# Attention and gated convolution on one core: five of seven slots of P through the DMA transpose, v scaled in its cast, row sums inverted before their transpose

## The chip, the core and the metric

The kernel runs on one core of a Trainium2 chip. The core has a matrix engine (TensorE, PE in the profile; its weight loads are PEld), a vector engine (VectorE, DVE), a scalar engine (ScalarE, ACT), a general one (GpSimd, POOL) and SyncE (SP), which here only issues DMAs. They work side by side and wait for one another by semaphores. Operands lie in SBUF; TensorE writes to PSUM, which has eight banks. The metric is the device time of one launch in microseconds.

## What is computed

For 8 batches and 12 heads of 448 tokens with 64 dimensions, q and k are normalised by their root mean square and multiplied by a gain; softmax attention gives x; x (448 x 768 a batch) goes through a matrix of 768 x 1024, a relu, a convolution of three taps along the tokens, a sigmoid gate, and a matrix of 1024 x 768.

```python
q_n, k_n = (rmsnorm(q, g_q), rmsnorm(k, g_k))
scores = scale * np.matmul(q_n, k_n.transpose(0, 1, 3, 2))
scores = scores - np.max(scores, axis=-1, keepdims=True)
attn = np.exp(scores)
attn = attn / (np.sum(attn, axis=-1, keepdims=True) + 1e-09)
out = np.matmul(attn, v)
...
h = np.maximum(x @ w_in, 0.0)
conv_out[t] = conv_w[0] * h[t - 1] + conv_w[1] * h[t] + conv_w[2] * h[t + 1]
gate = 1.0 / (1.0 + np.exp(-conv_out))
return h * gate @ w_out
```

## The kernel before

**Precision.** Most products run in fp16 with operands split in a cast and a remainder (names ending in `_hi` and `_lo`), three matmuls for one: high by high and the two mixed ones. An operand is scaled by a power of two first, so that the cast is safe. What stays in f32 is multiplied in f32 directly.

**Pairs, slots, groups.** The 96 heads go in 48 pairs n, six a batch. The 896 query rows of a pair are seven slots of 128. `SLOTS` (567) gives the order in which the slots are worked (index j) and `GROUPS` (568) which of them share a group of score matmuls. The first three groups hold two slots each, one from each head, and use the two halves of 64 rows of TensorE at once; the last holds slot 3 alone, which has rows of both heads, and uses all 128 rows with the operand `qz`, which `q_middle` (484) copies together on POOL or DVE. For each slot `soft_max` (602) takes the row maximum on DVE and `soft_exp` (608) the exponential on ACT, which also sums the row into a column of `rsum`. The exponentials go to a ring `e` of three buffers.

**P, turned in two ways.** The product with v needs P transposed. In the pairs before `n1` = 8 all seven slots are transposed on TensorE in f32 (`p_transpose`, 648, line 651 in the profile) and copied from PSUM to `PT` by ACT or DVE (`p_evac`, 655). From pair 8 on, the first nd = 4 slots take another way: `p_hi` (626) casts P to fp16, `p_lo` (634) makes the remainder, both in one of three buffers `ph`, and `p_turn` (641) has SP issue a DMA transpose of both into the other part of `PT`. `pv` (715) multiplies: eight f32 products (line 723) over the columns of the slots that TensorE turned, 192 of each head's 448 columns from pair 8 on, and 24 fp16 matmuls (line 732) over the other 256. The fp16 part needs v split as well: `v_scaled` (694) multiplies v by its power of two in place, on POOL or DVE, `v_hi` (700) casts it, `v_lo` (703) subtracts. The scale comes from the largest absolute value of v in the batch (`v_scale`, 547), and is taken out again behind the convolution and at the output.

**The sums.** When all seven slots are summed, `rsum` (128 x 7) is transposed on TensorE to 7 x 128 (666), `sum_evac` copies it out of PSUM and adds 1e-9 (671), `sum_inverse` takes the reciprocal on DVE (663), and SP writes it to DRAM and reads it back twice, spread over 64 partitions each (`rB`, 676 and 682). `x_scale` (740) multiplies the product by it; `x_hi` and `x_lo` split x.

**The rest.** q and k are loaded, squared, summed and scaled (`square`, `square_sum`, `rsqrt`, `apply_rms`), then transposed on TensorE (458) or, for q from pair 8 on, by DMA (`x_turn`, 451). When a batch's six pairs are done, `in_part` (800, line 806) and `out_part` (869, line 883) multiply by the two weight matrices, with the relu, the convolution, the gate and a split between. The weights come as 64-bit floats, which DVE unpacks with integer operations (`to_f32`, 205); they are then scaled and split (`split` on ACT, `rest` on DVE or POOL).

**The order of the work.** A planner in the kernel gives each step a due time (`at`, 141): pair n begins at `base(n)` (68), which is `T0` for each of the first `N0` pairs and `T` after that; other steps are due at fixed distances from it, and the weights between `wi0` and `wi1`, `wo0` and `wo1` (the constants of line 20). `needs` (989) says what a step waits for and `options` (1253) which engines can do it and at what cost, `PATIENCE` (1331) what a second choice is charged. A loop simulates the engines, picks at each moment the most urgent step that can start, and so writes the fixed order of each engine's instructions. DVE operations named in `SHARED` (1432) are planned so as not to overlap POOL's. SP's queue is in order too: a transfer that waits holds those behind it.

## Time and profile before

| | us |
|---|---|
| median of 3 runs | 926.09 |
| lowest, highest | 924.29, 948.67 |
| the profiled execution | 925.0 |
| its span, from first to last instruction | 923.2 |
| TensorE busy in the span | 849.0 |
| DVE, ACT, POOL busy | 730.2, 667.4, 627.3 |

The mean clock granted to TensorE was 0.972 of full speed. In a row of the groups stand the source line, the engine, the operation, the tiles that it writes and reads with their shapes, the number of instructions, then the busy time, the mean of one in ns, and the idle time of the engine before them with what ended it. A row in order of time begins with its start and its length. A row of waits names who waited for whom, then the sum, the count and the longest. A line can be that of a helper: 78 is every plain copy and cast, 90 every two-operand operation, so there the tiles tell which step it is.

### The profile page before, as it was taken

The numbers are of one execution on the slowest core, as the hardware profiler recorded it, in microseconds if no ns is written. First come the engines' busy times: TensorE is split into PE (matmuls) and PEld (weight loads), VectorE is DVE, ScalarE is ACT, GpSimd is POOL, SyncE is SP. The second block draws the span as 40 slices with busy tenths as digits, with TensorE's granted clock in tenths as the row PEclk, the third lists the DMA queues.
The fourth block names the chain that finished last, engine by engine and source line by source line (L and its number), as shares of the span: only waits on it lengthen the run. The fifth ranks groups of instructions, "written<-read, shape, count | busy, mean of one in ns | idle before, by whom it ended". The sixth has DMA issues, their size and how long they took to land.

```text
span 923.2 us, 18519 instructions
## 1 busy us (share of the span) xinstructions
PE 849.0 (92%) x6430; PEld 508.7 (55%) x6430; DVE 730.2 (79%) x1336; ACT 667.4 (72%) x1525; POOL 627.3 (68%) x705
## 2 busy tenths in 40 slices
PE   1686687998999999999999999999999999999998
PEld 0343344555656566556665566566655666566554
DVE  6998987999788887798798976898789876893330
ACT  3677776887688776788688877787788867885441
POOL 2396887787699768668688857777778755872120
PEclk9897787999999999999999999999999999999999
DMA  8934432376885878556976588568696695455001
GB/s 212 259 96 126 122 113 63 89 135 117 185 147 130 156 152 170 123 117 124 187 148 139 115 182 168 95 135 164 150 170 126 119 175 120 84 94 112 18 18 52
DMA packets 296878, 120.18 MB, mean 130 GB/s; under 512 B 258048, under 2 KB 293200, under 8 KB 296784
## 3 DMA queue, kind: packets, MB, share of 16 engines
q1 hardware_dynamic: 296784, 119.00, 62.1%
q8 instruction: 50, 0.82, 0.4%
q14 instruction: 44, 0.36, 0.1%
HBM read 56.65 MB, written 11.18 MB: 73 GB/s over the span
## 4 chain that ended last, share of the span: by engine, by line
PE 67%; DVE 18%; DMA 5%; ACT 4%; issue 2%; SPq 2%; POOL 2%; DVEq 0%; ACTq 0%; POOLq 0%
PE bank L883 19%; PE bank L806 19%; PE bank L600 9%; PE bank L723 7%; PE bank L651 6%; PE bank L732 4%; DMA rB<-rd 3%; PE bank L462 2%; DVE rT L663 1%; DMA v<-in_v_dram 1%; DVE st L365 1%; DVE wo L214 1%; POOL sq L90 1%; DVE vacc L528 1%; SPq L643 1%
## 5 line engine op out<-in xcount | busy, mean ns | idle before, releaser
L806 PE MATMUL bank<-x,wi 128*128 128x448 f16 x1152 | 241.9, 354 | 0.3 <-ACT e_(8_0_1731 L614 0.3
L883 PE MATMUL bank<-wo,gring 128*128 128x384 f16 (+1 forms) x1056 | 205.4, 327 | 0.7 <-DVE c_(4_7_8185 L839 0.3
L806 PEld LDWEIGHTS <-wi 128*128 128x128 f16 x1152 | 110.2, 98 | 99.8 <-issue 14.7
L883 PEld LDWEIGHTS <-gring 128*128 128x128 f16 (+1 forms) x1056 | 101.8, 99 | 62.7 <-issue 11.0
L78 ACT COPY PT<-bank 112x512 f32<-112x512 f32 x166 | 96.6, 586 | 42.9 <-PE bank L651 41.9
L600 PE MATMUL bank<-kT,qT 64*128 64x448 f16 x864 | 107.1, 370 | 1.2 <-ACT qT L78 0.6
L90 POOL TENSOR_TENSOR sq<-qkf,st 112x512 f32<-112x512 f32 x79 | 87.5, 1125 | 17.6 <-DVE st L387 15.6
L723 PE MATMUL bank<-PT,v 112*64 112x192 f32 (+1 forms) x768 | 88.8, 374 | 1.7 <-ACT PT L78 1.3
L90 POOL TENSOR_TENSOR x<-rB,x 128x448 f16<-128x448 f32 x48 | 51.5, 1073 | 47.5 <-ACT x L78 36.4
L723 PEld LDWEIGHTS bank<-PT,v 112*64 112x64 f32 x768 | 51.5, 138 | 34.5 <-issue 18.1
L600 PEld LDWEIGHTS <-qT 64*128 64x128 f16 x864 | 34.8, 97 | 49.4 <-issue 28.2
L365 DVE TENSOR_REDUCE st<-sq 112x16 f32<-112x1024 f32 x48 | 57.9, 1207 | 3.7 <-ACT sq L357 3.6
L732 PE MATMUL bank<-PT,vp 112*64 112x256 f16 x960 | 59.2, 273 | 0.0
L696 POOL TENSOR_SCALAR v<-v,vsc 112x512 f32<-112x512 f32 x35 | 57.6, 1649 | 1.9 <-DVE vsc L200 0.9
L732 PEld LDWEIGHTS <-vp 112*64 112x64 f16 x960 | 53.0, 110 | 2.6
L741 DVE TENSOR_TENSOR rB<-bank,rB 128x448 f32<-128x448 f32 x48 | 29.7, 619 | 29.4 <-DMA rB<-rd 20.7
L491 POOL COPY qz<-qT 64x128 f16<-64x128 f16 x88 | 33.2, 378 | 28.3 <-DMA qT<-qkf 17.2
L462 PE MATMUL bank<-ident,sq 112*128 112x112 f32 x224 | 33.6, 276 | 18.8 <-POOL sq L90 18.7
L90 POOL TENSOR_TENSOR vp<-v,vp 112x512 f16<-112x512 f32 x39 | 46.6, 1195 | 2.8 <-ACT vp L78 1.6
L883 PE MATMUL bank<-wo,wi 128*128 128x384 f16 (+1 forms) x192 | 46.9, 326 | 0.0
L663 DVE RECIPROCAL rT<-rT 7x128 f32<-7x128 f32 x48 | 44.9, 935 | 0.7
L90 POOL TENSOR_TENSOR qkf<-sq,qkf 112x512 f16<-112x512 f32 x29 | 35.0, 1208 | 13.8 <-ACT qkf L78 7.2
(2235 smaller groups left out, 2101.6 us busy)
## 6 DMA issues: line engine op xcount, KB each, us to landing
qkf<-in_k_dram SPq DMA_DIRECT2D x48, 224.0 KB
qkf<-in_q_dram SPq DMA_DIRECT2D x48, 224.0 KB
v<-in_v_dram SPq DMA_DIRECT2D x48, 224.0 KB
rB<-rd SPq DMA_DIRECT2D x96, 112.0 KB
wo<-in_moe_w_in_dram SPq DMA_DIRECT2D x12, 512.0 KB
gring<-in_moe_w_out_dram SPq DMA_DIRECT2D x16, 384.0 KB
PT<-ph SPq DMA_TRANSPOSE x160
rd<-rT SPq DMA_DIRECT2D x48, 3.5 KB
```

The lines of the kernel that those rows point to most:

```text
L78: (nc.scalar.copy if e == "ACT" else elementwise(e).tensor_copy)(dst, src)
L90: elementwise(e).tensor_tensor(dst, a, b, op=op)
L365: nc.vector.tensor_reduce(old("st", m)[:, 0, n - m].rearrange("p i s -> p (i s)"), old("sq", n).rearrange("p i h t d -> p (i h t) d"), axi ...
L462: nc.tensor.transpose(ps[:, t * PB : (t + 1) * PB], x[:, t], ident[:PB, :PB])
L600: nc.tensor.matmul(ps[u][:, :S], lhs, kt[r, w], start=(i == 0), stop=(i == 2))
L651: nc.tensor.transpose(ps[:PB, kt * P : (kt + 1) * P], e[:, kt * PB : (kt + 1) * PB], ident)
L663: nc.vector.reciprocal(old("rT", n), old("rT", n))
L696: elementwise(on["v_scaled", n]).tensor_scalar(v, v, old("vsc", n // NP)[:PB, 1:2], None, op0=ALU.mult)
L723: nc.tensor.matmul(ps[HALF[h], out[h]], v[:, h, k], pt[:, k, col[h]], start=(k == 0), stop=(k == NB - 1),)
L732: nc.tensor.matmul(ps[HALF[h], out[h]], v[:, w, h, k], pt[:PB, a, k, col[h]], start=(i == 0 and k == 0), stop=(i == 2 and k == NB - 1),)
L806: nc.tensor.matmul(ps[:, :S], wi[:, wl, c, fc * P : (fc + 1) * P], old("x", b * NP + c)[:, xl], start=(i == 0), stop=(i == 3 * NP - 1),)
L883: nc.tensor.matmul(ps[p0 : p0 + m, :NO2], g, wo[:, wl, fc, half * NO2 : (half + 1) * NO2], start=(i == 0), stop=(i == 3 * NFC - 1),)
```

## The change

From pair 10 on instead of pair 8, five slots in place of four go through the DMA transpose (`dg` is now that number); the slots are worked in the order 2, 4, 1, 5, 3, 0, 6, so that 0 and 6, the first rows of one head and the last of the other, stay on TensorE. Slot 3 is now the fifth in the order, and its group the third of four. The f32 product covers 128 columns a head from pair 10 on, the fp16 one 320.

`v_scaled` is gone. The scale of v is applied in the cast (`v_hi`) and in the remainder, which is now always on DVE as (v x scale) - cast. The f32 product takes v as loaded, so its slots lack the scale: `sum_evac` multiplies the inverted sums by the scale for these slots and by one for the others, from a column of `vsc` that `v_scale` fills with one more small operation, from two masks made once in `prepare`.

The sums are completed (`sum_add`, on ACT, DVE or POOL) and inverted as 128 x 7, then transposed and evacuated.

The constants of the planner are changed with it (`T0` and `N0`, `T`, the weights' times, the charges of second choices), `x_cast`, `x_hi`, `in_hi` and `p_hi` may go to POOL too, `scores` waits for `q_middle` only in the group of slot 3, and options that were switched off (`xin`, `gin`, `ein`) are taken out.

```diff
-    T0=18.19, N0=5, T=16.2, ti=26.722, si=4.889, so=6.734, hop=0.568, beta=0.028, wi0=-41.512,
-    wi1=117.871, wo0=38.32, wo1=134.629, cw=-29.146, p_evac=1.201, p_hi=2.093, p_lo=5.553,
...
-    sp=0.107, nbulk=5, p_rs=0.005, p_sq=0.945, p_w=0.508, v0=-5.896, dg=2, n1=8, sw=0, pvs=4,
+    T0=16.073, N0=6, T=15.869, ti=26.722, si=4.889, so=6.219, hop=0.568, beta=0.028, wi0=-40.836,
+    wi1=117.871, wo0=31.379, wo1=166.21, cw=-27.026, p_evac=1.19, p_hi=1.894, p_lo=5.553,
...
+    p_ev=8.767, sp=0.066, nbulk=4, p_rs=0.005, p_sq=0.939, p_w=0.414, v0=-5.839, dg=5, n1=10,
+    sw=0, pvs=2, pk=0.1, p_sa=0.167, p_ph=0.399, p_pl=0.756, nq=8, nk=99, p_qh=0.524, p_ql=0.275,
...
     def v_scale(b):
...
         pow2_scale(sc[:, 0:1], sc[:, 1:2])
+        nc.vector.scalar_tensor_tensor(
+            sc[:NS, 6:7], raw_slot[:NS], sc[:NS, 1:2], cast_slot[:NS], op0=ALU.mult, op1=ALU.add
+        )
...
-    SLOTS = (0, 6, 1, 5, 2, 4, 3)
-    GROUPS = ((0, 1), (2, 3), (4, 5), (6,))
+    SLOTS = (2, 4, 1, 5, 3, 0, 6)
+    GROUPS = ((0, 1), (2, 3), (4,), (5, 6))
...
-        return 0 if n < PH["n1"] else 2 * PH["dg"]
+        return 0 if n < PH["n1"] else PH["dg"]
...
+    def sum_add(n):
+        r = old("rsum", n)
+        if on["sum_add", n] == "ACT":
+            nc.scalar.activation(r, r, AF.Identity, bias=tiny)
+        else:
+            elementwise(on["sum_add", n]).tensor_scalar(r, r, 1e-9, None, op0=ALU.add)
+
     def sum_inverse(n):
-        nc.vector.reciprocal(old("rT", n), old("rT", n))
+        nc.vector.reciprocal(old("rsum", n), old("rsum", n))
...
     def sum_evac(n):
-        nc.vector.tensor_scalar(
-            new("rT", n, [NS, P], F32), bank("t", ("r", n))[:NS, :P], 1e-9, None, op0=ALU.add
+
+        w = 6 if nd(n) else 1
+        copy_scaled(
+            on["sum_evac", n], new("rT", n, [NS, P], F32), bank("t", ("r", n))[:NS, :P],
+            old("vsc", n // NP)[:NS, w : w + 1],
         )
...
-    def v_scaled(n):
-        v = old("v", n).rearrange("p h t d -> p (h t d)")
-        elementwise(on["v_scaled", n]).tensor_scalar(
-            v, v, old("vsc", n // NP)[:PB, 1:2], None, op0=ALU.mult
         )
 
     def v_hi(n):
-        copy(on["v_hi", n], new("vp", n, [PB, 2, 2, NB, D], F16)[:, 0], old("v", n))
+        copy_scaled(
+            on["v_hi", n], new("vp", n, [PB, 2, 2, NB, D], F16)[:, 0], old("v", n),
+            old("vsc", n // NP)[:PB, 1:2],
+        )
 
     def v_lo(n):
         vp = old("vp", n)
-        binary(on["v_lo", n], vp[:, 1], old("v", n), vp[:, 0], ALU.subtract)
+        nc.vector.scalar_tensor_tensor(
+            vp[:, 1], old("v", n), old("vsc", n // NP)[:PB, 1:2], vp[:, 0], op0=ALU.mult,
+            op1=ALU.subtract,
+        )
...
         elif name == "scores":
             for h in range(2):
                 yield ("x_turn" if turned(n, h) else "qk_lo"), n, h
-                yield "q_middle", n, h
+                if a[1] == 2:
+                    yield "q_middle", n, h
```

More of the change, by code (lines that the diff above doesn't have):

```diff
@@ L611, in soft_exp @@
         c = SLOTS[j]
-        if not inside(n, j):
-            new("e", (n, j), [P, S], F32)
         nc.scalar.activation(
-            powers(n, j), bank("s", (n, j))[:, :S], AF.Exp, bias=old("sst", (n, j)),
+            new("e", (n, j), [P, S], F32), bank("s", (n, j))[:, :S], AF.Exp, bias=old("sst", (n, j)),
             accum_out=old("rsum", n)[:, c : c + 1],
         )
-    def inside(n, j):
-        return PH["ein"] and j < nd(n)
-    def powers(n, j):
-        return bank("s", (n, j))[:, :S] if inside(n, j) else old("e", (n, j))
     def p_hi(n, j):
@@ L735, in pv @@
                 )
-    def x_place(n):
-        return bank("m", ("v", n))[:, :S] if PH["xin"] else old("rB", n)
     def x_scale(n):
-        nc.vector.tensor_tensor(x_place(n), bank("m", ("v", n))[:, :S], old("rB", n), op=ALU.mult)
+        t = old("rB", n)
+        nc.vector.tensor_tensor(t, bank("m", ("v", n))[:, :S], t, op=ALU.mult)
     def x_hi(n):
-        copy(on["x_hi", n], new("x", n, [P, 2, S], F16)[:, 0], x_place(n))
+        copy(on["x_hi", n], new("x", n, [P, 2, S], F16)[:, 0], old("rB", n))
     def x_lo(n):
         xt = old("x", n)
-        binary(on["x_lo", n], xt[:, 1], x_place(n), xt[:, 0], ALU.subtract)
+        binary(on["x_lo", n], xt[:, 1], old("rB", n), xt[:, 0], ALU.subtract)
     def plan_attention(n):
@@ L1169, in needs @@
             yield "sum_store", n
[L1170 removed]
+            yield "x_lo", n - BUFS["rB"]
             if a[1]:
@@ L1339, in takes @@
         if name == "scores":
-            return "s", [((a[0], j), ("p_lo" if inside(a[0], j) else "soft_exp", a[0], j)) for j in GROUPS[a[1]]]
+            return "s", [((a[0], j), ("soft_exp", a[0], j)) for j in GROUPS[a[1]]]
         if name == "qk_transpose":
@@ L1350, in takes @@
             return "t", [(("x", a[0]), ("v_scale", *a))]
-        if name == "pv" and not a[1]:
-            return "m", [(("v", a[0]), ("x_lo" if PH["xin"] else "x_scale", a[0]))]
+        if name == "pv" and a[1] == pvs(a[0])[0]:
+            return "m", [(("v", a[0]), ("x_scale", a[0]))]
         if name == "in_part" and not a[-2]:
-            return "m", [(("i", *a[:2]), ("in_lo" if PH["gin"] else "in_gate", *a[:2]))]
+            return "m", [(("i", *a[:2]), ("in_gate", *a[:2]))]
         if name == "out_part" and not a[-2]:
@@ L1357, in takes @@
         if name == "in_conv" and not a[-1]:
-            return "c", [(None, ("in_gate" if PH["gin"] else "in_lo", *a[:2]))]
+            return "c", [(None, ("in_lo", *a[:2]))]
         if name == "out_evac":
@@ L1402, in mode @@
     def mode(name, *a):
-        return name if name == "pv" or name == "scores" and a[1] < NG - 1 else ""
+        return name if name == "pv" or name == "scores" and a[1] != 2 else ""
     taken = {step: takes(*step) for step in steps}
@@ L1432, in tile_attention_moe @@
     SHARED = (
-        "apply_rms", "apply_gain", "x_cast", "x_rest", "p_lo", "p_hi", "v_lo", "v_hi", "v_scaled",
+        "apply_rms", "apply_gain", "x_cast", "x_rest", "p_lo", "p_hi", "v_lo", "v_hi", "sum_add",
         "x_hi", "x_lo", "in_hi", "in_lo", "in_carry", "q_middle", "convert", "rest", "moe_scales", "rsqrt",
     )
-    shared = set(SHARED)
-    for key, names in dict(xin=("x_hi", "x_lo"), gin=("in_hi", "in_lo"), ein=("p_hi", "p_lo")).items():
-        if PH[key]:
-            shared -= set(names)
     port = dict(DVE=0.0, POOL=0.0)
     def locks(e, name):
-        return e == "POOL" or e == "DVE" and name in shared
+        return e == "POOL" or e == "DVE" and name in SHARED
     BULK = ("load", "load_k", "load_q", "v_load")
```

129 lines of the change are left out of this document (66 added, 63 removed).

## The prediction

> **What bounds the kernel now.** I read the first two parts of the page, then the busy times by stretch, then TensorE's rows in order of time, then the groups by line and the waits.
>
> ```profile
> span 923.2 us, 18519 instructions
> PE 849.0 (92%) x6430; PEld 508.7 (55%) x6430; DVE 730.2 (79%) x1336; ACT 667.4 (72%) x1525; POOL 627.3 (68%) x705
> q1 hardware_dynamic: 296784, 119.00, 62.1%
> ...
> 25.00:175.00 150.00, 114.80 (x643) 61.74 (x644) 134.99 (x250) 108.98 (x255) 111.85 (x118) 0.83 0.47 121
> 175.00:200.00 25.00, 25.00 (x174) 13.14 (x172) 24.63 (x42) 22.32 (x53) 23.26 (x31) 1.00 0.65 119
> 200.00:250.00 50.00, 45.15 (x363) 28.41 (x363) 43.66 (x86) 37.52 (x88) 36.30 (x37) 1.00 0.75 151
> 250.00:850.00 600.00, 590.84 (x4777) 364.21 (x4773) 493.66 (x901) 466.37 (x1071) 440.22 (x497) 1.00 0.71 139
> 850.00:923.00 73.00, 68.54 (x464) 39.23 (x462) 16.52 (x25) 24.00 (x43) 9.32 (x9) 1.00 0.09 34
> ```
>
> The columns of a stretch are its length, then the busy time of PE, PEld, DVE, ACT and POOL, the granted clock, the DMA share and GB/s. There are two regimes. From 250 to 850 us PE works 590.84 of 600 us at clock 1.00, while DVE has 18% left, ACT 22%, POOL 27%: there the span is PE's work. From 25 to 175 us PE stands idle for 150 - 114.80 = 35.2 us, its clock is 0.83, and DVE is busy for 134.99 of 150, the fullest of all: there DVE sets the pace, for it also unpacks and splits the weights. The profiled execution took 925.0 us, 1.8 more than its span and 1.1 less than the median of 926.09; the sum below is made against 925.0.
>
> **TensorE's terms.** Ends of matmuls are modelled and overlap, so I take distances between starts.
>
> ```profile
> 401.94 1.52 PE L723 MATMUL bank<-PT,v 112*64 112x192 f32 x16
> 403.29 1.48 PE L732 MATMUL bank<-PT,vp 112*64 112x256 f16 x24
> 404.71 0.74 PE L600 MATMUL bank<-kT,qT 64*128 64x448 f16 x6
> 405.38 1.88 PE L806 MATMUL bank<-x,wi 128*128 128x448 f16 x9
> ...
> 411.08 0.60 PE L651 MATMUL bank<-ident,e_(21_5_5148 128*112 128x128 f32 x4
> 411.52 1.30 PE L806 MATMUL bank<-x,wi 128*128 128x448 f16 x6
> ...
> 413.29 1.31 PE L600 MATMUL bank<-kT,qT 64*128 64x448 f16 x12
> 414.53 0.60 PE L462 MATMUL bank<-ident,sq 112*128 112x112 f32 x4
> ...
> 60.64 3.23 PE L723 MATMUL bank<-PT,v 112*64 112x448 f32 x16 [1.31 <-ACT PT L78]
> ```
>
> - A slot of P moved from PE to the DMA saves four transposes, 411.52 - 411.08 = 0.44 us. 38 pairs (10 to 47) send one more: -16.7. Pairs 8 and 9 send none instead of four: 8 x 0.44 = +3.5.
> - The f32 product of P and v falls from 192 to 128 columns a head. From 448 to 192 columns it fell by 3.23 - 1.52 = 1.71, 6.7 ns a column, so 64 fewer save 0.43: x38 = -16.2. Pairs 8 and 9 return to 448: 2 x 1.71 = +3.4. Should weight loads, which don't shrink, set part of the pace, the saving is less; its ends are 0 and 16.2.
> - The f16 product grows from 256 to 320 columns. It takes 404.71 - 403.29 = 1.42 now; in proportion +0.36, x38 = +13.5, and pairs 8 and 9 drop it: -2.8. Its ends are 0 (if weight loads set its pace) and 13.5; I take the upper, since 24 matmuls in halves of 256 columns have little else to wait for.
> - The full-height group of scores (the single slot) moves from last to third, so the half-height groups are split once more a pair. Twelve half-height matmuls in a row take 414.53 - 413.29 = 1.24, six take 405.38 - 404.71 = 0.67: a split costs 0.10, or 0 where other work already stood between. I take half: 48 x 0.05 = +2.4, ends 0 and 4.8. The f32 product is now issued in two steps (pvs 2); both are ready at once, so I expect them back to back, 0, with the same upper end of 4.8.
>
> [...]
>
> PE's sum is -16.7 + 3.5 - 16.2 + 3.4 + 13.5 - 2.8 + 2.4 = -12.9 us. The bounds above give -26.4 - 2.4 at the one end (f16 product free, no splits) and +5.7 at the other (f32 product saving nothing, every group split), neither likely, since weight loads that set the pace would hit both products, -12.9 + 16.2 - 13.5 = -10.2.
>
> **VectorE, GpSimd, ScalarE.**
>
> ```profile
> L663 DVE RECIPROCAL rT<-rT 7x128 f32<-7x128 f32 x48 | 44.9, 935 | 0.7
> L536 DVE TENSOR_SCALAR vsc<-vsc 128x1 f32<-128x1 f32 x8 | 1.2, 154 | 0.3
> L696 POOL TENSOR_SCALAR v<-v,vsc 112x512 f32<-112x512 f32 x35 | 57.6, 1649 | 1.9 <-DVE vsc L200 0.9
> L696 DVE TENSOR_SCALAR v<-v,vsc 112x512 f32<-112x512 f32 x13 | 7.2, 550 | 0.0
> L90 POOL TENSOR_TENSOR vp<-v,vp 112x512 f16<-112x512 f32 x39 | 46.6, 1195 | 2.8 <-ACT vp L78 1.6
> L90 DVE TENSOR_TENSOR vp<-v,vp 112x512 f16<-112x512 f32 x1 | 1.5, 1531 | 0.0
> L301 DVE SCALAR_TENSOR_TENSOR wo<-wo,wsc 128x768 f16<-128x768 f32 x8 | 9.6, 1203 | 1.7 <-ACT wo L293 1.6
> L214 DVE SCALAR_TENSOR_TENSOR wo<-gring,wo 128x384 int32<-128x384 int32 x16 | 12.7, 795 | 0.3
> ...
> L671 DVE TENSOR_SCALAR rT<-bank 7x128 f32<-7x128 f32 x48 | 13.2, 274 | 16.0 <-PE bank L666 15.9
> L78 ACT COPY PT<-bank 112x512 f32<-112x512 f32 x166 | 96.6, 586 | 42.9 <-PE bank L651 41.9
> ...
> 25.00:175.00 150.00, 6.89 (x8) 0.83 0.47 121
> ...
> 25.00:175.00 150.00, 17.91 (x10) 0.83 0.47 121
> ```
>
> The last two rows are the reciprocals on DVE and the scaling of v on POOL between 25 and 175 us.
>
> - Reciprocal: 935 ns for 128 elements a partition. With 7 a partition it lies between the 154 ns of the one-element row and 274, the next row of this chain; I take 0.2. Saving 48 x 0.735 = 35.3. The new addition of 1e-9 costs 0.15 (by the 154 ns) wherever it is put; the evacuation after the transpose replaces the one before it, 0.27 for 0.27.
> - Scaling of v: 57.6 on POOL and 7.2 on DVE go. The scale comes into the cast of v (a scaled copy instead of a copy, no change of length taken; ends 0 and +0.1 a pair) and into the evacuation of the sums.
> - Remainder of v: 46.6 leaves POOL; 38 come to DVE as an operation of two SBUF inputs and a scale. Nearest rows: 795 ns at 384 and 1203 at 768 columns, so 0.93 at 512; the single remainder already on DVE took 1.53. 38 x 0.93 = 35, ends 27 and 58.
> - Remainders of P: 30 more (190 for 160) at about 1.05, +31 on POOL; 30 more casts on ACT (0.56, in the next fence) replace 30 evacuations (0.59).
>
> After 175 us DVE thus changes by about -30 - 7 - 2 + 35 + 6 = +2 us, at the worst end +25, against 106 us free; POOL by -40 - 47 + 31 = -56, so it can take the casts that the planner may now send it. Nothing here becomes the bound, and I cost all of it at nothing: PE's matmuls cover it. So too the first two groups of scores, which need not wait for the middle copies any more (no row of PE's waits names these), and five small operations in the preparation, 0.15 us each, before PE's first work.
>
> **The start.** Eight reciprocals lie in 25 to 175 us: -5.9 on DVE, +1.2 for the additions, -4.7 in all. The due times spread the second weight matrix over 134.8 us instead of 96.3, from 31.4 in place of 38.3, in 26 steps; the remainders start 16.5 steps and 6 us in, now at 105, the last before pair 8's 139.6, and then at 123, against pair 8's 128.2, so that 7 of the 8 (1203 ns each) come due at pair 8 or after: 8.4 us moved to where DVE has room. POOL loses 17.9 there, which only makes it a freer helper. DVE's relief is 13.1 of 134.99 us. The products of a batch's first pairs need not wait for the scale of v any more, only the sums do; that hides in the same pace. If DVE alone sets this pace, pair 8 starts that much sooner; if waits from engine to engine do, not at all. I take the removed 4.7 whole and half of the moved 8.4: -9. Ends 0 and -15.
>
> **DMA and SP.**
>
> ```profile
> L643 SPq DMA_TRANSPOSE PT<-ph x160: 1231/1259/3034, 174.3 to 844.5; - x160
> SPq L643 <- POOL ph L90: 53.3, 42, 2.4
> ACT ph L78 <- DMA PT<-ph: 6.8, 8, 1.9
> L78 ACT CAST ph<-e_(9_1_2017 x1: 560/560/560, 193.4 to 193.4; 128x448 f16<-128x448 f32 x1
> L90 POOL TENSOR_TENSOR ph<-e_(8_1_1789,ph x1: 1047/1047/1047, 177.9 to 177.9; 128x448 f16<-128x448 f32 x1
> 331.28 3.16 DMA rB<-rd
> ...
> L614 ACT ACTIVATE e_(8_0_1731<-bank,sst_(8_0_1713 x1: 631/631/631, 170.3 to 170.3; 128x448 f32<-128x448 f32 x1
> ...
> PE bank L462 <- POOL sq L90: 18.7, 2, 18.3
> PE bank L651 <- ACT e_(2_6_736 L614: 3.8, 1, 3.8
> ```
>
> 30 more transposes hold SP for 30 x 1.26 = 38 us over 670, and each carries 128 x 1024 two-byte values, 262 kB. At the queue's rate, 119 MB in 62.1% of 923.2 us or 208 GB/s, that is 1.26 us each, so 38 us more of the 16 engines, 0.71 to 0.77 of the stretch; if all DMA time were transposes (479 us in 200 of them, 2.4 each) it is 72 us, to 0.82. Either fits. On SP a transpose waits for its remainder (42 waits, 1.27 us each), and loads and the store of the sums queue behind it; 38 such waits more can cost PE nothing while its row of waits after 250 us names no transfer. I cost it at 0, and likewise that four bulk loads at once are planned instead of five.
>
> **Sum.** 925.0 - 12.9 - 9 = 903.1, so 903: 2.5% under the median.
>
> **Rivals.**
>
> A, the start gains more. PE waits there on casts, exponentials and POOL (the last two rows above), each of which DVE or POOL feeds; with all 13.1 plus POOL's relief it is -15, and a busier PE would also regain clock. Between 25 and 175 us 17% of 114.80 busy us, 19.5, is lost to the lower clock; idle cut by 15 of 35.2 would return up to 43% of that, 8; I take 5. 925.0 - 12.9 - 20 = 892.
>
> [...]
>
> B, the start gains nothing, because chains from engine to engine set it: PE's terms alone, 912, within 2%. For it: the longest single wait, 18.3 us, is before the first pair, out of reach.
>
> C, slower: the ring of three buffers of the split P holds ACT. One trip of a buffer is cast 0.56, remainder 1.05, wait 1.27, issue 1.26, landing about 3.2 (the sums' broadcast above), 7.3 us; three buffers serve five slots in 12.2 us, against a pair's 670.2 / 39.75 = 16.9 us now (159 intervals of four). The ring decides once a trip takes 16.35 x 3 / 5 = 9.8 us; then ACT waits, with the exponentials queued behind it, and PE's transposes and scores behind those. At 11 us a pair takes 18.3: 903 + 38 x 1.95 = 977. It ends slower by 2% from 10.5 us on. For it: ACT already waited for the ring 8 times, 6.8 us; against it: that is 8 of 160.
>
> D, the f32 product saves nothing at 128 columns, weight loads setting its pace: 903 + 16.2 = 919, within 2%.
>
> **How the numbers follow.** Forecast (895 to 911) 0.50, A 0.17, B 0.20, C 0.05, D 0.08. Two per cent, about what a measurement of this kernel can tell from no change, ends at 907.6 and 944.6. Below 907.6 lie A and 0.42 of the forecast's 0.50: faster 0.59. B, D and the rest: same 0.36. C: slower 0.05. The range reaches over the forecast, A's middle and B, and part of D: 890 to 917, leaving out half of A's tail, C and most of D.
>
> **What would show it.** Right: L651 at 584 records (10 x 28 + 38 x 8), rows of L723 at 112x128 near 1.1 us and L732 at 112x320 near 1.8; PE still above 97% busy from 250 to 850; pair 8's exponentials, now at 170 us, some 9 us sooner; reciprocals near 0.2 us; POOL about 70 us less busy in all. Wrong: PE rows of waits naming P's transfers, or ACT waiting for the ring by tens of us (C); pair 8 no sooner (B); L723 still at 1.5 (D).

## The result, and the profile after

The changed kernel takes 887.7 us (median of 4 runs, 886.3 to 888.4), against 925.8 us for the kernel before in the same comparison: a ratio of 0.959, with a 95% interval of 0.957 to 0.961. It is faster by 4.1%. The prediction was 903.0 us with a range of 890 to 917, so the direction was right and the time lies 2.3 us below the range. The profiled execution took 888.4 us.

The head of the changed kernel's page, with the span, TensorE's row of busy times and the DMA queue, answers to the first three lines shown of before:

```profile
span 886.0 us, 18318 instructions
PE 829.4 (94%) x6262; PEld 476.7 (54%) x6262; DVE 701.1 (79%) x1288; ACT 678.9 (77%) x1593; POOL 609.1 (69%) x738
q1 hardware_dynamic: 328464, 126.87, 68.8%
```

The busy times by stretch of the changed kernel, with the same columns as before:

```profile
25.00:175.00 150.00, 124.49 (x755) 66.44 (x752) 133.97 (x266) 125.01 (x309) 109.53 (x123) 0.92 0.48 129
175.00:200.00 25.00, 25.00 (x159) 12.77 (x158) 22.53 (x43) 22.55 (x52) 22.77 (x22) 1.00 0.30 67
200.00:250.00 50.00, 49.55 (x397) 30.07 (x396) 45.16 (x77) 39.05 (x95) 40.97 (x50) 1.00 0.93 189
250.00:850.00 600.00, 595.58 (x4713) 346.97 (x4713) 480.95 (x863) 477.96 (x1115) 427.77 (x526) 1.00 0.77 151
850.00:886.00 36.00, 31.41 (x236) 18.74 (x230) 2.04 (x4) 6.88 (x12) 2.07 (x2) 1.00 0.12 45
```

TensorE's busy time fell by 849.0 - 829.4 = 19.6 us and its idle time by 74.2 - 56.6 = 17.6 us. The prediction had put 12.9 us on the first and 9 on both together in the start. Between 25 and 175 us idle fell from 35.2 to 25.5 us and the clock rose from 0.83 to 0.92; from 250 to 850 us idle fell from 9.2 to 4.4 us.

A better cut is by pairs, for the same pair is the same work. These are the first exponentials of pairs 8, 10 and 45 in the changed kernel (the start stands after "to"):

```profile
L618 ACT ACTIVATE e_(8_0_1744<-bank,sst_(8_0_1727 x1: 633/633/633, 154.1 to 154.1; 128x448 f32<-128x448 f32 x1
...
L618 ACT ACTIVATE e_(10_0_2227<-bank,sst_(10_0_2211 x1: 634/634/634, 192.8 to 192.8; 128x448 f32<-128x448 f32 x1
...
L618 ACT ACTIVATE e_(45_0_10755<-bank,sst_(45_0_10732 x1: 640/640/640, 764.5 to 764.5; 128x448 f32<-128x448 f32 x1
```

And of pairs 10 and 45 in the kernel before, where pair 8 stood at 170.3:

```profile
L614 ACT ACTIVATE e_(10_0_2222<-bank,sst_(10_0_2210 x1: 622/622/622, 207.2 to 207.2; 128x448 f32<-128x448 f32 x1
...
L614 ACT ACTIVATE e_(45_0_10897<-bank,sst_(45_0_10885 x1: 635/635/635, 802.3 to 802.3; 128x448 f32<-128x448 f32 x1
```

| stretch | before | after | difference | the prediction's terms |
|---|---|---|---|---|
| to pair 8 | 170.3 | 154.1 | -16.2 | -9, and 8 splits of 0.05 = +0.4 |
| pairs 8 and 9 | 36.9 | 38.7 | +1.8 | +3.5 + 3.4 - 2.8 + 0.1 = +4.2 |
| pairs 10 to 44 | 595.1 | 571.7 | -23.4 | 35 x (-0.44 - 0.43 + 0.36 + 0.05) = -16.1 |
| pair 45 to the end | 120.9 | 121.5 | +0.6 | -1.4 |
| span | 923.2 | 886.0 | -37.2 | -21.9 |

Two stretches gave more than predicted: the start by 7.6 us and pairs 10 to 44 by 7.3. The busy times of exactly this second stretch tell the two kinds of gain apart. Before:

```profile
207.20:802.30 595.10, 583.46 (x4726) 359.68 (x4724) 497.74 (x917) 462.91 (x1063) 444.45 (x500) 1.00 0.72 142
```

After:

```profile
192.80:764.50 571.70, 566.91 (x4547) 331.48 (x4546) 485.83 (x876) 468.72 (x1104) 434.35 (x538) 1.00 0.84 164
```

TensorE's busy time fell by 16.5 us, near the prediction's 16.1 (how near is taken up below). Its idle time fell from 595.10 - 583.46 = 11.6 to 4.8 us, and of that the prediction had nothing.

### The profile page after: what moved, and what is told of

Its sections match the earlier page's. It is cut to its first block, busy times and chain, and to the rows that moved or that the text cites. A ratio compares the mean times of both kernels' runs of the same rounds, so it can differ in the third digit from the quotient of the medians.

```text
span 886.0 us, 18318 instructions
## 1 busy us (share of the span) xinstructions
PE 829.4 (94%) x6262; PEld 476.7 (54%) x6262; DVE 701.1 (79%) x1288; ACT 678.9 (77%) x1593; POOL 609.1 (69%) x738
## 4 chain that ended last, share of the span: by engine, by line
PE 66%; DVE 15%; DMA 5%; POOL 5%; ACT 3%; issue 2%; SPq 1%; ACTq 0%; POOLq 0%; DVEq 0%
PE bank L889 21%; PE bank L814 17%; PE bank L606 9%; PE bank L733 6%; PE bank L742 5%; PE bank L649 5%; DMA PT<-ph 2%; DMA rB<-rd 2%; PE bank L465 1%; POOL ph L90 1%; DMA qT<-qkf 1%; POOL sq L90 1%; DVE st L368 1%; DVE vacc L531 1%; DVE wi L217 1%
## 5 line engine op out<-in xcount | busy, mean ns | idle before, releaser
L78 ACT COPY PT<-bank 112x512 f32<-112x512 f32 x142 | 82.8, 585 | 22.3 <-PE bank L649 21.8
L90 POOL TENSOR_TENSOR sq<-qkf,st 112x512 f32<-112x512 f32 x84 | 95.4, 1154 | 6.3 <-DVE st L390 3.7
L733 PE MATMUL bank<-PT,v 112*64 112x128 f32 (+1 forms) x768 | 76.0, 335 | 1.1 <-DVE rB L749 0.5
L742 PE MATMUL bank<-PT,vp 112*64 112x320 f16 x912 | 69.8, 300 | 0.7 <-DMA PT<-ph 0.7
L733 PEld LDWEIGHTS bank<-PT,v 112*64 112x64 f32 x768 | 43.3, 137 | 30.7 <-issue 19.0
L742 PEld LDWEIGHTS <-vp 112*64 112x64 f16 x912 | 49.6, 110 | 18.8 <-issue 7.6
L465 PE MATMUL bank<-ident,sq 112*128 112x112 f32 x224 | 32.5, 268 | 20.2 <-POOL sq L90 19.8
L494 POOL COPY qz<-qT 64x128 f16<-64x128 f16 x88 | 32.2, 365 | 27.1 <-DMA qT<-qkf 13.7
L465 PEld LDWEIGHTS bank<-ident,sq 112*128 112x128 f32 x224 | 25.1, 143 | 29.0 <-POOL sq L90 22.5
L712 DVE SCALAR_TENSOR_TENSOR vp<-v,vsc,vp 112x512 f16<-112x512 f32 x38 | 39.7, 1047 | 0.5 <-ACT vp L82 0.4
L90 POOL TENSOR_TENSOR qkf<-sq,qkf 112x512 f16<-112x512 f32 x31 | 37.2, 1201 | 2.8 <-ACT qkf L78 2.2
L606 PE MATMUL bank<-kT,qz 128*128 128x448 f16 x144 | 36.7, 365 | 1.6 <-DVE rB L749 1.6
```

The source lines that it names most:

```text
L78: (nc.scalar.copy if e == "ACT" else elementwise(e).tensor_copy)(dst, src)
L90: elementwise(e).tensor_tensor(dst, a, b, op=op)
L465: nc.tensor.transpose(ps[:, t * PB : (t + 1) * PB], x[:, t], ident[:PB, :PB])
L494: e.tensor_copy(z[HALF[h], :, HALF[h]], old("qT", n)[HALF[h], :, t0 : t0 + 64])
L606: nc.tensor.matmul(ps[u][:, :S], lhs, kt[r, w], start=(i == 0), stop=(i == 2))
L712: nc.vector.scalar_tensor_tensor(vp[:, 1], old("v", n), old("vsc", n // NP)[:PB, 1:2], vp[:, 0], op0=ALU.mult, op1=ALU.subtract,)
```

## The experiments

Times are given as the ratio to the kernel before on the same chip (it ran between 922.1 and 925.8 us there); 0.001 is 0.93 us. "Idle" is TensorE's idle time in the stretch from pair 10 to pair 45, worked out from a row like the two above.

**How far does the order alone move the time?** Each experiment that changes a step or a constant makes the planner write another order for every engine. Two runs of the changed kernel and one of the kernel before measured this with a change of one constant that means nothing; a fourth gave the planner truer durations for two steps.

```diff
e13, changed kernel:  -beta=0.028   +beta=0.0285
e14, changed kernel:  -hop=0.568    +hop=0.572
e15, kernel before:   -beta=0.028   +beta=0.0285
e16, changed kernel:
-            sum_add=lambda: [act(0.25), dve(0.17), pool(0.26)],
+            sum_add=lambda: [act(0.3), dve(0.62), pool(0.44)],
...
-            v_lo=lambda: [dve(0.73)],
+            v_lo=lambda: [dve(1.05)],
```

> The changed kernel with one constant of the planner, beta, at 0.0285 in place of 0.028: no operation, no due time and no charge of a second choice changes, but the fixed order of all engines is written anew. If the undo runs measured their parts, an arbitrary other order costs little: 885 to 891 us, pair 8 at 153 to 156 us, pairs 10 to 45 in 571 to 574 us. If a good part of what they cost (6 to 19 us) was only that the order was no longer the one that the constants had been fitted to, this run too goes up, to 894 to 900 us.

> The changed kernel with hop at 0.572 in place of 0.568, a second arbitrary order from pair 6 or so on. The same alternatives: 885 to 891 us if the parts were measured, 894 to 900 us if the order alone costs that much. Together with the run at beta 0.0285 it gives the size below which an undo run tells nothing of its part.

> The kernel before with beta at 0.0285 in place of 0.028. If the constants of the kernel before were fitted to its order, it goes up by 5 us or more, to over 930 us, as a kernel with arbitrary constants would; if its order is nothing special, it stays within 4 us of 925 us. Its pairs 10 to 45, 595.1 us in the kernel before, tell whether the gaps of TensorE there are those of one order (then this moves by 5 us or more either way) or of the planned reciprocal (then 592 to 598 us).

> The changed kernel with the planned durations of two of its own operations set near what its trace shows: v's remainder on DVE 1.05 us in place of 0.73, the addition to the sums 0.30 on ACT, 0.62 on DVE and 0.44 on POOL in place of 0.25, 0.17 and 0.26. If a plan with true durations leaves TensorE fewer gaps, as the kernel before with the reciprocal at 0.94 did, pairs 10 to 45 go from 571.7 to some 569 us and the time to 884 us; if the order's scatter is larger than this, it comes out anywhere between 885 and 900 us.

The three orders of the changed kernel came out at 0.9635 [0.9591, 0.9679], 0.9610 [0.9576, 0.9643] and 0.9667 [0.9632, 0.9702], against 0.9592: 2 to 7 us slower, though only the last is clear of the intervals (the four executions of the first alone lie between 888.1 and 895.7 us). Pair 8 starts at 155.4, 152.2 and 155.2 us, pairs 10 to 44 take 575.6, 575.7 and 573.5 us, idle is 6.9, 7.1 and 5.6 us. The kernel before with another order: 0.9995 [0.9974, 1.0017], pair 8 at 175.8 us, pairs 10 to 44 in 591.1 us, idle 7.7:

```profile
209.60:800.70 591.10, 583.38 (x4712) 360.00 (x4713) 497.43 (x914) 463.56 (x1066) 441.24 (x499) 1.00 0.74 144
```

So an order is worth up to 7 us in these runs, and a run within that of the changed kernel tells nothing of the part that it undid. True durations did not make the changed kernel faster.

Even one order doesn't always take the same time. Up to pair 8 the changed kernel and three of the runs below (the one with more work on VectorE in pairs 10 to 45, and seven slots with three and with four buffers) give TensorE, VectorE and ScalarE the same instructions in the same order, and GpSimd too but for one memset more in two of them. Pair 8 starts at 154.1, 153.1, 152.4 and 150.3 us there. These are the rows up to pair 8 of the second and of the last; the changed kernel's stands further below:

```profile
25.00:153.10 128.10, 105.88 (x628) 56.00 (x625) 113.47 (x229) 106.01 (x264) 89.30 (x111) 0.91 0.50 140
...
25.00:150.30 125.30, 104.11 (x626) 55.33 (x623) 112.04 (x230) 105.83 (x264) 90.08 (x110) 0.90 0.50 140
```

So 4 us at pair 8 can be nothing but another execution, on the same chip or another. The changed kernel's other orders differ from it by less there; the other order of the kernel before, by 5.5.

**All constants of the planner.** The changed kernel, with every constant and step cost of the kernel before (for steps that both have), and all new operations:

```diff
-    T0=16.073, N0=6, T=15.869, ti=26.722, si=4.889, so=6.219, hop=0.568, beta=0.028, wi0=-40.836,
+    T0=18.19, N0=5, T=16.2, ti=26.722, si=4.889, so=6.734, hop=0.568, beta=0.028, wi0=-41.512,
...
-            p_evac=lambda: [act(0.59), dve(0.68)],
+            p_evac=lambda: [act(0.65), dve(0.69)],
...
```

> The changed kernel with the planner's constants and the step costs of before (due times T0, N0, T, so, the weights' windows, the charges of second choices, pvs 4, no option of POOL for the casts of q, x, gate); five slots, v's scale in its cast and the sums' new order stay. Theory 'order' (pair 8 starts 16 us sooner because due times place the weights' work later and the pairs sooner): the start's gain goes, pair 10's first exponential moves from 192.8 us to 205 or later, and the time is 900 to 906. Theory 'relief' (the start gains because the scaling of v and the long reciprocal are gone from POOL and DVE, whatever the constants): 886 to 893, pair 10 at 190 to 197.

Measured: 0.9806 [0.9775, 0.9837]; the profiled span is 904.1 us, 18.1 more than the changed kernel's. Pair 8 starts at 165.7 us (+11.6), pairs 10 to 44 take 577.6 us (+5.9). The stretch from pair 10 to 45:

```profile
204.40:782.00 577.60, 566.33 (x4548) 334.40 (x4547) 480.66 (x869) 469.65 (x1110) 429.73 (x522) 1.00 0.82 162
```

TensorE is busy as long as in the changed kernel (566.3 to 566.9), and idle as long as in the kernel before (11.3 to 11.6). So in this stretch the busy time goes with the new operations. The idle time went with the constants in this one pair of runs; the kernel before itself leaves 4.5 to 11.6 us in the three orders run here, so that the constants as such cause it isn't shown. The reverse, the operations of before under the new constants, was not run. From the kernel before to this run the span falls by 19.1 us, which is close to the prediction's sum without its 4.2 for the moved weights, 21.9 - 4.2 = 17.7.

**Which constants?** Of those, once only the due times, once only the charges and step costs, and once only the window of the second weight matrix were set back.

```diff
e9:  T0=18.19, N0=5, T=16.2, so=6.734, wi0=-41.512, wo0=38.32, wo1=134.629, cw=-29.146, v0=-5.896
e10: p_hi=2.093, p_rms=1.879, p_qz=0.982, nbulk=5, pvs=4, ... (the rest, with the step costs)
e8:  wo0=38.32, wo1=134.629
```

> The changed kernel with the due times of before alone (T0, N0, T, so, both weights' windows, cw, v0); the charges and costs stay new. Of the 18 us that e1_old_constants lost, 12 were lost by pair 10 (192.8 us to 204.4). Theory 'due times' (how early pairs are due against the weights decides the start): pair 10 at 200 or later, time 897 to 906. Theory 'charges' (which engine takes the casts, evacuations and remainders decides it): pair 10 within 3 us of 192.8, time 887 to 893.

> The changed kernel with the charges for second choices and the planned costs of before (no option of POOL for the casts, pvs 4, four or five bulk loads as before); the due times stay new. Theory 'due times': 887 to 893, pair 10 within 3 us of 192.8. Theory 'charges': pair 10 at 200 or later, 897 to 906.

> The changed kernel with the second weight matrix due between 38.3 and 134.6 as before, not 31.4 and 166.2; nothing else changed. Theory 'weights' window' (the prediction's 8.4 us of DVE work moved past pair 8): pair 10 later by 6 to 11 us, time 894 to 899. Theory 'other constants': pair 10 within 3 us of 192.8, time 886 to 891.

Measured: due times 0.9844 [0.9794, 0.9894], pair 8 at 160.9 us, idle 8.7; charges 0.9734 [0.9699, 0.9768], pair 8 at 159.1, idle 10.7; window 0.9665 [0.9621, 0.9709], pair 8 at 156.1, idle 8.0. In the start the two halves add up to the whole, 6.8 + 5.0 = 11.8 of 11.6, which may be chance, since either is hardly more than another order or execution moves. (The profiled execution with the old due times lay 6 us below their median.) The window is inside what another order does; the prediction's 4.2 us for it isn't shown.

**Five slots against four.** The changed kernel with four slots from pair 10 on, in the old order and groups:

```diff
-    p_ev=8.767, sp=0.066, nbulk=4, p_rs=0.005, p_sq=0.939, p_w=0.414, v0=-5.839, dg=5, n1=10,
+    p_ev=8.767, sp=0.066, nbulk=4, p_rs=0.005, p_sq=0.939, p_w=0.414, v0=-5.839, dg=4, n1=10,
...
-    SLOTS = (2, 4, 1, 5, 3, 0, 6)
-    GROUPS = ((0, 1), (2, 3), (4,), (5, 6))
+    SLOTS = (0, 6, 1, 5, 2, 4, 3)
+    GROUPS = ((0, 1), (2, 3), (4, 5), (6,))
...
```

> The changed kernel with four slots through the DMA from pair 10 on, with the slots' order and groups of before; constants, sums and v as changed. By the prediction's TensorE terms 0.44 + 0.43 - 0.36 - 0.05 = 0.46 us a pair come back: pairs 10 to 45 take 16 us more, 588, and the time is 903 to 907. If VectorE's and the planner's share is larger than TensorE's, fewer: 890 to 897.

Measured: 0.9750 [0.9707, 0.9794], with pair 8 at 151.5 us. The stretch from pair 10 to 45:

```profile
191.00:777.30 586.30, 582.90 (x4692) 356.38 (x4690) 475.62 (x857) 470.15 (x1108) 428.00 (x535) 1.00 0.70 145
```

Busy is the 583 us of the kernel before, idle 3.4: with four slots TensorE is busy for 99.4% of this stretch, and only less work helps there. The fifth slot takes 582.90 - 566.91 = 16.0 us of it, as the prediction's terms say. It also brings 0.14 of DMA share; 1.4 us of idle more are within what an order does.

**From pair 8 or from pair 10.** The same change from pair 8 on should save two more pairs of TensorE work.

```diff
-    ... dg=5, n1=10,
+    ... dg=5, n1=8,
```

> The changed kernel with five slots through the DMA from pair 8 on, not from pair 10. By the prediction's terms TensorE is spared 2 x (5 x 0.44 + 2.14 - 1.78) = 5 us, so 883 if TensorE alone counts there. Theory 'start is short of POOL and DVE': the ten casts, ten remainders and two splits of v on ACT, POOL and DVE in the start make up for it or more: 887 to 895.

Measured: 0.9664 [0.9632, 0.9696]. Pair 8 starts at 152.0 us, but pairs 8 and 9 take 41.9 us in place of 38.7 and idle is 7.4. No gain is shown, and no loss beyond what an order does.

**The sums and v, undone one at a time.** The sums transposed first and inverted as 7 x 128 again, once planned at 0.28 us as in the kernel before and once at 0.94, which is what it takes; and v scaled in place with its remainder on POOL or DVE. The diff shows the main lines of each.

```diff
e3, e6:
-        nc.vector.reciprocal(old("rsum", n), old("rsum", n))
+        nc.vector.reciprocal(old("rT", n), old("rT", n))
...
-            sum_inverse=lambda: [dve(0.19)],
e3:
+            sum_inverse=lambda: [dve(0.28)],
e6:
+            sum_inverse=lambda: [dve(0.94)],
e4:
+        elementwise(on["v_scaled", n]).tensor_scalar(
+            v, v, old("vsc", n // NP)[:PB, 1:2], None, op0=ALU.mult
...
-        nc.vector.scalar_tensor_tensor(
-            vp[:, 1], old("v", n), old("vsc", n // NP)[:PB, 1:2], vp[:, 0], op0=ALU.mult,
-            op1=ALU.subtract,
-        )
+        binary(on["v_lo", n], vp[:, 1], old("v", n), vp[:, 0], ALU.subtract)
...
```

> The changed kernel with the sums as before: transposed first, then 1e-9 added, the scale of v divided out in the same operation, and the reciprocal taken on 7 x 128, planned at the cost that the planner of before gave it. Theory 'the reciprocal's relief of DVE matters in the start': 0.74 us more on DVE in each of 10 pairs there, pair 10 later by 5 to 8 us, time 892 to 898. Theory 'order': pair 10 within 3 us of 192.8, time 886 to 891, since TensorE covers the rest.

> The changed kernel with the old sums (as e3_old_sums), the reciprocal planned at 0.94. Theory 'misplanned': most of the 19 us of e3 comes back, 888 to 895, pairs 10 to 45 in 571 to 576 us. Theory 'DVE time': 900 to 907, as e3.

> The changed kernel with v scaled in place on POOL or DVE and its remainder on POOL or DVE, as before; the sums stay inverted first and get no scale. Theory 'relief of POOL matters in the start' (17.9 us of scaling there): pair 10 later by 5 to 10 us, time 893 to 900. Theory 'order': within 3 us, 886 to 891. In the PE-bound part POOL gains some 87 us and DVE loses 40, which both should cost nothing.

Measured: 0.9802 [0.9771, 0.9833] with the sums undone, and in its stretch from pair 10 to 45

```profile
197.30:782.80 585.50, 568.25 (x4529) 330.46 (x4526) 511.21 (x883) 463.82 (x1058) 439.38 (x547) 1.00 0.82 160
```

idle is 17.3 us, with DVE busy for 511 of 585.5; pair 8 starts at 155.1 us, 1.0 later. Planned at the true length: 0.9751 [0.9702, 0.9800], pair 8 at 161.0 us, idle 11.2 (in an execution 5.6 us above the median). With a median of 900.5 us it gets back 5 to 6 of the 19 us and misses what "misplanned" expected. The old v: 0.9724 [0.9675, 0.9773], pair 8 at 160.9 us, idle 10.1; its time, 899.4 us, is as "relief of POOL" expected, with pair 10 later by 4.7 us, just short of its 5 to 10; but 4.7 us there, and 6.8 at pair 8, are hardly more than orders and executions make. From pair 10 to 45 most of the loss is idle time on TensorE; its busy time rises only from 567 to between 568 and 570. Undone one at a time, the sums, v, the constants and the fifth slot cost more together than the whole change gave (19.4 + 12.2 + 19.8 + 14.6 = 66 of 38 us, from the ratios), so they can't be read as separate parts: either they overlap, or some of them contain a plan that no longer fits.

**The kernel before, its plan told the truth.** Only the planned length of the reciprocal is changed, no operation.

```diff
-            sum_inverse=lambda: [dve(0.28)],
+            sum_inverse=lambda: [dve(0.94)],
```

> The kernel before, with one number changed: the planner charges the reciprocal of 7 x 128 with 0.94 us, as measured, instead of 0.28. What is computed and every instruction's length stay; only the order can change. Theory 'misplanned': in the old-sums run pairs 10 to 45 took 585.5 us against 571.7 because the fixed order expects DVE 0.65 us a pair earlier than it is, and TensorE waits in that order; then planning it right brings before down by 6 to 15 us, to 910 to 919. Theory 'DVE time': the 0.74 us itself lies in the way; then the time stays within 4 us of before.

Measured: 0.9981 [0.9964, 0.9998]. Pairs 10 to 44 take 586.8 us, 8.3 less than in the kernel before and 4.3 less than in its other order, with idle at 4.5 us; but pair 8 starts at 178.7 us, 8.4 later:

```profile
213.30:800.10 586.80, 582.32 (x4719) 358.39 (x4719) 492.08 (x908) 457.69 (x1060) 455.44 (x509) 1.00 0.74 145
```

The idle time of the kernel before in these pairs was thus no property of its operations alone. But in both of its other orders the start lost about what the middle gained, and the time stayed: no run here has its operations with fewer gaps and no later start, and "misplanned", which expected 910 to 919 us, missed (922.6). That the true length is the cause is not shown: the other order came half the way with no reason at all.

**The same order, with more work on VectorE.** These two keep the changed kernel's order on every engine and add one reciprocal of 7 x 128 on a tile that nobody reads, behind the real one, in pairs 0 to 7 (e17) or 10 to 45 (e18); the planner doesn't know of it.

```diff
-        nc.vector.reciprocal(old("rsum", n), old("rsum", n))
+        nc.vector.reciprocal(old("rsum", n), old("rsum", n)); (0 <= n < 8) and nc.vector.reciprocal(spin, spin)
...
```

> The changed kernel in its own order of all engines; after the reciprocal of pairs 0 to 7 VectorE takes one more of 7 x 128 elements on a tile of ones that nobody reads, unknown to the planner: 8 x 0.94 = 7.5 us of VectorE between 25 and 154 us. If VectorE alone paces the start, pair 8 starts 6 to 8 us later, at 160 to 162 us, and the time is 893 to 896 us. If chains from engine to engine pace it, as the prediction's rival B had it, pair 8 stays within 2 us of 154 and the time within 2 us of 887.7 us. At the prediction's half it is 3 to 4 us.

> The same addition to pairs 10 to 45 in place of 0 to 7: 36 x 0.94 = 33.7 us more of VectorE in some 590 us in which it has 15 per cent free, in the changed kernel's own order. The prediction costed such work at nothing there: pairs 10 to 45 in 570 to 574 us and the time at 886 to 890 us. My theory from the kernel before with its reciprocal planned at the true length is that work that the planner does not count opens gaps on TensorE, a quarter of its length: pairs 10 to 45 in some 580 us, the time at 894 to 898 us. If VectorE were the bound there, it would be 33 us more, 921 us.

In the start it came to 7.1 us of VectorE, by the groups of that run:

```profile
L668 DVE RECIPROCAL spin<-spin 7x128 f32<-7x128 f32 x8 | 7.1, 890 | 0.0
...
25.00:156.70 131.70, 109.51 (x629) 57.37 (x626) 117.62 (x237) 106.37 (x265) 89.69 (x111) 0.88 0.48 136
```

Pair 8 starts at 156.7 us, 2.6 to 6.4 later than in the four executions of the same order without this work; the time is 890.1 us, 2.3 more than the changed kernel's 887.7, or 5.8 by the ratios (0.9655 [0.9633, 0.9676]). So between 0.4 and 0.9 of the added work shows at pair 8: VectorE's work delays the start, but whether by the prediction's half or nearly whole these runs don't tell. The delay is not idle time: TensorE is idle for 22.2 us in this row, against 21.2 to 25.2 in those four, and busy for 4 to 6 us longer at a lower clock, 0.88 against 0.90 to 0.92. The trace's clock record, which has only the values 0.5 and 1.0 here, shows 30.6 us at 0.5 before pair 8, and 20.4 to 23.9 in those four. The second run added 32.0 us; its stretch from pair 10 to 45:

```profile
191.80:768.30 576.50, 567.97 (x4547) 331.02 (x4546) 516.33 (x910) 469.73 (x1105) 436.79 (x538) 1.00 0.83 163
```

VectorE is busy 30.5 us longer, TensorE idle for 8.5 us in place of 4.8, and the stretch is 4.8 us longer; the time is 892.0 us, 4.3 more, or 7.1 by the ratios (0.9669 [0.9653, 0.9686]). Such work wasn't free in the part that TensorE bounds: it cost 0.13 to 0.22 of its length (in the first run, whose pairs 10 to 44 have the changed kernel's instructions in its order, that stretch took 570.5 us with idle at 3.6, so an execution alone makes up some 1 us of the 4.8).

**The ring of the split P.** All seven slots through the DMA transpose, with three buffers and with four:

```diff
e11: -dg=5  +dg=7
e12: -dg=5  +dg=7    -ph=3  +ph=4
```

> The changed kernel with all seven slots through the DMA from pair 10 on, three buffers for the split P. TensorE would be spared 0.88 of transposes and the f32 product's 1.02 us a pair, less 0.66 for wider fp16 matmuls: 1.24 x 38 = 47, so 841 if TensorE alone decides. Theory 'DMA engines' (0.84 busy at 16.3 us a pair, 13.7 us of work, two more transposes of 1.26 make 16.2): no gain, 880 to 892. Theory 'ring' (rival C: seven trips of 7.3 us through three buffers, 17.0 us a pair): 910 to 920, and ACT waits for the ring by over 100 us.

> The same with four buffers for the split P. Theory 'ring': seven trips through four buffers are 12.8 us a pair, so the ring no longer decides, and the time falls by 20 us or more against three buffers. Theory 'DMA engines': within 8 us of the run with three buffers, the DMA share in the middle 0.95 or more in both.

Measured: 1.0733 [1.0695, 1.0772] with three buffers, slower than before, and 1.0190 [1.0146, 1.0234] with four. TensorE has less to do, but it waits, and its clock falls to 0.92 and 0.95; with three buffers, a stretch and two rows of waits:

```profile
250.00:500.00 250.00, 214.79 (x1399) 105.98 (x1399) 190.25 (x349) 180.76 (x419) 181.56 (x213) 0.92 0.84 169
...
ACT ph L78 <- DMA PT<-ph: 27.3, 42, 1.7
PE bank L742 <- DMA PT<-ph: 23.3, 14, 6.4
```

With four:

```profile
250.00:500.00 250.00, 227.82 (x1494) 114.20 (x1493) 204.99 (x368) 193.94 (x454) 192.02 (x224) 0.95 0.92 180
...
ACT ph L78 <- DMA PT<-ph: 59.2, 65, 2.3
```

One more buffer gives 50 us, so with three the ring was the limit, at seven slots: a pair takes 666.6 / 35 = 19.0 us there, 17.6 with four buffers. "Ring" expected 17.0 us a pair, 910 to 920 us in all, and ScalarE waiting for over 100 us; the time was 991 us, and ScalarE's own row of waits for the ring is 27 us, less than with four buffers. So it is the 50 us, and not this row, that shows the ring; where it holds up the engines wasn't followed. With four the transfers are near full, at 0.92 to 0.94. The prediction's rival C is a real mechanism, two slots further on.

## Why the prediction was wrong, step by step

**TensorE's terms** were right in the main. The rows of the changed kernel in order of time, for the two products:

```profile
422.13 1.09 PE L733 MATMUL bank<-PT,v 112*64 112x128 f32 x16
423.16 0.82 PE L889 MATMUL bank<-wo,gring 128*128 128x384 f16 x4
...
427.08 1.82 PE L742 MATMUL bank<-PT,vp 112*64 112x320 f16 x24
428.83 0.93 PE L606 MATMUL bank<-kT,qT 64*128 64x448 f16 x8
```

The f32 product takes 423.16 - 422.13 = 1.03 us from start to start; before, it was 403.29 - 401.94 = 1.35, so it saved 0.32 and not 0.43. The f16 product takes 1.75, 0.33 more than its 1.42, where 0.36 was taken. With the transposes at 0.44 that is 0.43 us a pair for the predicted 0.46. The split of the score groups, taken as 0.05 a pair, hardly came: from pair 10 to 45 the half-height matmuls stand in 75 runs in place of 71. From pair 8 to the end the busy time fell by 11.7 us (733.9 to 722.2) for a predicted 4.2 - 16.1 - 1.4 = -13.3. That 16.5 came so close to 16.1 from pair 10 to 45 is partly luck: the stretch holds 12 matmuls of `in_part` and 6 of the scores fewer than before, some 3 us by the distances above, which ran outside it. Rival D, an f32 product that saves nothing, is out.

**The start** was mis-sized, and this is the first step that failed. "I take the removed 4.7 whole and half of the moved 8.4: -9" let the planner's constants act through the weight matrix alone, and the 16.2 us measured lie beyond even its end of 15. The relief of VectorE itself was forecast nearly right, 13.1 us where 15.8 were measured: the reciprocals up to pair 8 took 1.4 us in place of 6.5, and two remainders of the second weight matrix in place of seven fell to VectorE there (of the other six, one ran on VectorE and five on GpSimd, all after pair 8). VectorE's remainders up to pair 8, before and after:

```profile
L301 DVE SCALAR_TENSOR_TENSOR wo<-wo,wsc 128x768 f16<-128x768 f32 x7 | 8.6, 1232 | 1.7 <-ACT wo L293 1.6
...
L304 DVE SCALAR_TENSOR_TENSOR wo<-wo,wsc 128x768 f16<-128x768 f32 x2 | 2.2, 1077 | 0.3 <-ACT wo L296 0.3
```

What went wrong is the half: pair 8 came sooner by about as much as VectorE was relieved. That VectorE's relief is the whole reason isn't shown. With all constants of before, the new operations take 7.0 us off VectorE and bring pair 8 from 170.3 to 165.7, -4.6, about the 4.7 of the reciprocals; with the reciprocals alone undone pair 8 starts only 1.0 later. The constants bring 11.6 more, and the weights' window alone is not to be told from another order. The two stretches up to pair 8 show what is gained; before:

```profile
25.00:170.30 145.30, 110.45 (x619) 59.28 (x619) 130.29 (x243) 104.57 (x246) 108.59 (x116) 0.82 0.48 125
```

and after:

```profile
25.00:154.10 129.10, 103.87 (x628) 55.07 (x625) 114.45 (x229) 106.30 (x264) 90.75 (x110) 0.91 0.51 139
```

TensorE's idle time fell from 34.9 to 25.2 us, -9.6, and its busy time by 6.6 us for about as many matmuls (619 and 628 records), while the clock went from 0.82 to 0.91, which in proportion would be worth 110.45 x (1 - 0.82 / 0.91) = 10.9, an estimate. That matmuls took longer at the lower clock the kernel before shows: the four transposes of a slot of P took 48.19 - 47.29 = 0.90 us from start to start where its clock was 0.50, and 54.59 - 54.16 = 0.43 where it was 1.00. The regained clock is rival A's second term, taken there as 5; that a busier TensorE brought it is not shown, for two other runs had 22 us of idle time at a clock of 0.88. VectorE worked 15.8 us less, GpSimd 17.8 less and ScalarE 1.7 more. Of what the chip did here, rival A (892 us) came nearest. Whether by its reason, DVE's relief with POOL's, stays open: the old v, which gives POOL its work back, starts pair 8 6.8 us later, but under the constants of before the new operations gained only 4.6.

**"I cost all of it at nothing: PE's matmuls cover it"** is the second step that failed. The cover had holes, 9.2 us of TensorE's idle time from 250 to 850 us, which stood in the quoted row and was read as fixed. Between pairs 10 and 45 they were 11.6 us, and the changed kernel closed 6.8 of them. That this idle time depends on the plan, and not on the operations alone, is what the runs show: the new operations under the old constants leave 11.3 us of it, as the kernel before does; an old way of the sums or of v under the new constants leaves 10 to 17, and four slots 3.4; the kernel before, planned anew with hardly a change, 7.7 and 4.5; the changed kernel in four orders 4.8 to 7.1. What VectorE's lighter work contributes by itself is bounded by the run that put 32 us back: 0.13 to 0.22 of its length. Where the prediction had "+2 us" for VectorE after 175 us, it worked 13 us less from pair 8 to the end (583.2 to 570.2; 4 less in the run with work added in the start alone, which has the same instructions there). At 0.22 that is at most 3 us of the gain. GpSimd, forecast at -56 us after 175 us and some -70 in all, worked 18 us less in all and no less from pair 8 on: the new plan gave it other work, such as 174 remainders of P in place of 131.

**Single durations.** These groups of the changed kernel answer to the rows that they were taken from:

```profile
L668 DVE RECIPROCAL rsum<-rsum 128x7 f32<-128x7 f32 x48 | 9.3, 195 | 5.1 <-ACT rsum L663 4.5
L712 DVE SCALAR_TENSOR_TENSOR vp<-v,vsc,vp 112x512 f16<-112x512 f32 x38 | 39.7, 1047 | 0.5 <-ACT vp L82 0.4
L82 ACT ACTIVATE vp<-v,vsc 112x512 f16<-112x512 f32 x36 | 25.7, 718 | 6.1 <-PE bank L742 6.1
L663 ACT ACTIVATE rsum<-rsum,tiny 128x7 f32<-128x7 f32 x32 | 9.7, 304 | 0.4
L665 DVE TENSOR_SCALAR rsum<-rsum 128x7 f32<-128x7 f32 x9 | 5.6, 618 | 2.6 <-ACT e_(17_6_4079 L618 1.4 <-ACT e_(11_6_2615 L618 0.5 <-ACT e_(45_6_10975 L618 0.5
```

The reciprocal takes 195 ns for the 0.2 us taken, v's remainder 1.05 us for 0.93, inside its ends of 27 and 58 us in all. The addition to the sums went mostly to ScalarE, at 304 ns for the 0.15 taken.

**The ring and the transfers** held: ScalarE waits for the ring 31 times, 21.1 us in all, in place of 8 times and 6.8, which is at the edge of the prediction's own sign for rival C ("tens of us"); but TensorE waits for P's transfers only 0.7 us, so it cost little.

```profile
ACT ph L78 <- DMA PT<-ph: 21.1, 31, 2.9
...
PE bank L742 <- DMA PT<-ph: 0.7, 2, 0.4
```

**Pairs 8 and 9** cost 1.8 us of the predicted 4.2, within what an order does. Rival B, a start that gains nothing, is out by its time; its reason, waits from engine to engine, may still be a part of the pace.

What stays open is how much of the start's gain is VectorE's relief, and which of the due times and charges close which hole: each set alone is undone with a new order, and 7 us of such a difference may be the order's. No version tried was faster than the changed kernel.

## What to carry to other kernels

When a change comes with new constants for whatever orders the work, bound what the new order may give by the idle time of the engine that bounds each stretch, here 35 us in the start and 9 after 250 us, and let the range reach for it; a cover of matmuls with holes is no cover. Cut two traces at the same pair of work, not at the same microsecond, and split each stretch into busy and idle: here busy time followed the operations to two or three microseconds, and idle time moved with the plan. Before an undone part is read, run the kernel in an arbitrary other order, and the same order more than once; here an order alone was 2 to 7 us, and one order alone scattered by 4 us at pair 8.
